# Finding the tokens of fixed expert items by comparisons and small products instead of a round trip through a slot table

## The chip, the cores and the metric

One core of a Trainium2 chip runs one program: three stages in a row, attention, a dense feed-forward layer and a top-1 mixture of experts. The metric is the device time of one execution in microseconds (us); lower is better. The profile is of one execution of the same program.

## The reference

Inputs are q, k, v of 2 batches x 8 heads x 576 positions x 64. The attention has a rotary position turn; its output is a matrix x of 1152 tokens x 512. The part that matters here is what follows the dense layer:

```python
x = _moe_ref(x, w_in, w_out)            # 1152 x 512 -> 2048 -> 512, gelu by sigmoid
logits = x @ w_gate                     # 8 experts
expert_idx = np.argmax(logits, axis=1)
gate_w = softmax(logits)[arange(N), expert_idx]
for i in range(N):                      # in order of the tokens
    e = expert_idx[i]
    if counts[e] < capacity:            # capacity = 288
        disp[e, counts[e]] = x[i]; pos[i] = counts[e]; counts[e] += 1; keep[i] = True
h = np.maximum(einsum('ecd,edf->ecf', disp, w1), 0)
y = einsum('ecf,efd->ecd', h, w2)       # 512 -> 1024 -> 512
out[i] = gate_w[i] * y[expert_idx[i], pos[i]] if keep[i] else 0
```

## The kernel before

**Matrix products.** A float32 operand is split into a rounded high part and a remainder (`hl[:, 0]`, `hl[:, 1]` for weights, `gh`, `gl` for activations), and each product is done three times: high by high, high by low, low by high. ScalarE writes the high part of a weight slice (L833), VectorE the low part (L834). A ring of four slices holds them.

**Order.** A planner orders the attention by hand. From the dense layer on the code is written in program order, and a scheduler that simulates the engines lays each engine's instructions out in one fixed sequence. Each engine works through its own sequence in order.

**Dense layer** (`first`, L904). The tokens go through in three chunks, 0 to 512, 512 to 768 and 768 to 1152 (`CUTS`). Each chunk makes 16 slices of the hidden layer: 12 products `h` (L853) and, two slices later, the products `y` (L883). The rows are written to a table in HBM, `x2`, one for each batch of 576 tokens.

**Routing** (`route`, L979). After the second chunk all tokens of batch 0 are known, after the third those of batch 1. For each batch some 60 small VectorE operations and six small products (`rank`, L1020 and L1023) give each token a slot number `lin`: the two largest groups of a batch become *items*. Four items are fixed: items 0 and 1 of batch 0 with 3 blocks of 96 and 2 blocks of 112 slots, items 2 and 3 of batch 1 with 3 blocks of 96 and 1 block of 96 (`STATIC`). What doesn't fit goes to surplus items, at most 16, in a loop at the end that runs `n - 4` times. In the profiled execution the loop doesn't run: there are nine gathers (L1146) and nine sends (L1193), one for each fixed block.

**The way from slot number to rows.** `route` casts `lin` to integers (`at`, L1056) and makes an `entry` for each token: its row in `x2` for the one batch and the other, its output row, its gate. Ten indirect DMAs issued by GpSimd (POOL in the profile; L1069, five for each batch, one for each tile of 128 tokens) scatter the entries into a table in HBM, `slots`. `gather` (L1136) reads an item's entries back (`ent`, L1141) and uses them as indices of an indirect DMA that fetches the tokens' rows (`got`, L1146; four buffers). `turn` (L1157) turns the rows on TensorE into `xt`.

**Experts** (`second`, L1205, for items 0 to 2; `few`, L1224, for item 3). Each item runs 8 slices through `h` and `y`; item 0 and 2 with 288 columns, item 1 with 224. A *hook* is a piece of work put into the sequence of slices: `turn(1)` and `turn(3)` four slices before the end of the items 0 and 2, `turn(2)` at the end of the last slice of item 1. The result `y` is copied to `yt` (L1213, one buffer), turned back (L1218), multiplied by the gate (L1221) and sent to the output rows by an indirect DMA (`send`, L1193). Which expert an item has is read from a small table `etab` that `route` fills after the slot numbers.

Of the kernel before, what the change touches and what calls it, by code (L numbers as in the profile page):

```python
# [25 lines left out]
P = 128  # L26
# [9 lines left out]
ROWS = 20  # L36
NSLOT = ITEMS * HALF
# [180 lines left out]
def consts():  # L218
# [18 lines left out]
    for b in range(B):  # L237
        rows[:, :, :, b] = np.where(batch == b, c, FAR)
    rows[:, :, :, 2] = batch * S + c
    masks = np.concatenate([valid.reshape(P, -1), (FAR * (1 - valid)).reshape(P, -1)], axis=1)  # L240
# [15 lines left out]
        "before": np.triu(np.ones((P, P), np.float32), 1),  # L256
        "small": np.repeat(small.astype(np.float32)[None], P, 0),
# [454 lines left out]
class Experts:  # L712
# [42 lines left out]
    def prepare(self):  # L755
# [19 lines left out]
        self.oh = one.tile([P, NC + 1, E], BF16, name="r_oh")  # L775
        self.small = one.tile([P, NC * E + 2 * ROWS * E + ROWS], F32, name="small")
# [202 lines left out]
    def route(self, b, L):  # L979
# [44 lines left out]
        rank, cnt = rank[:, 0:NC], rank[:, NC]  # L1024
        left, kc, items, key, base, at0 = (each(n) for n in ("left", "kc", "items", "key", "base", "at0"))
# [32 lines left out]
        ls, ex, sm, gate = big("ls"), big("ex"), col("sm"), col("gate")  # L1058
        tt(ls, L, per(mx), ALU.subtract)
        nc.scalar.activation(out=ex, in_=ls, func=AF.Exp)  # L1060
        red(sm, ex)
        ts(sm, sm, 1e-9, ALU.add)
        v.reciprocal(out=gate, in_=sm)
# [3 lines left out]
        done = []  # L1067
        for j in range(NC):
            ins = nc.gpsimd.indirect_dma_start(  # L1069
                out=self.slots,  # L1070
                out_offset=bass.IndirectOffsetOnAxis(ap=at[:, j:j + 1], axis=0),
                in_=entry[:, j, :],
                in_offset=None,
                bounds_check=NSLOT - 1,
                oob_is_err=False,
            )
            for x in done:
                self.tc.declare_no_dep(ins.ins, x.ins, reason="each token has a slot of its own")
            done.append(ins)
# [55 lines left out]

    def gather(self, item, batches, blocks=3, size=TT):  # L1136
# [6 lines left out]
        for i in range(blocks):  # L1143
            row = self.three.tile([P, DM], F32, name="got", bufs=4)[0:size]
            for b in batches:
                nc.gpsimd.indirect_dma_start(  # L1146
                    out=row,
                    out_offset=None,
                    in_=self.x2[b],
                    in_offset=bass.IndirectOffsetOnAxis(ap=ent[:, i, b:b + 1], axis=0),  # L1150
                    bounds_check=S - 1,
                    oob_is_err=False,
                )
# [51 lines left out]
    def second(self, ent, x, expert, hook=None):  # L1205
# [4 lines left out]
        y = self.ffn(x, [lambda f=f: self.slice_of(expert, f) for f in range(F2 // P)], self.relu, {hook[0]: hook[1]} if hook else {})  # L1210
# [96 lines left out]
    def run(self):  # L1307
        nc, tc = self.nc, self.tc
        sp = [mybir.EngineType.SP]
        found, x = {}, {}  # L1310

# [3 lines left out]
        def known(k):  # L1315
# [4 lines left out]
            for i in range(2 * b, 2 * b + 2):  # L1320
                found[i] = self.gather(i, [b], *STATIC[i])
# [8 lines left out]
        for i in range(3):  # L1330
            self.second(found[i][0], x[i], self.expert(i, sp), ((4, 0, 4)[i], lambda: turn(i + 1)))
        self.few(found[3][0], x[3], self.expert(3, sp))
        n = nc.values_load(self.etab[0:1, ITEMS:ITEMS + 1], min_val=4, max_val=ITEMS)
        with tc.If(n > 4, label="more"), tc.For_i(4, n, 1, iteration_sync="staggered") as i:
            ent, rows = self.gather(i, [0, 1])
            tc.stage_boundary()
            self.cut = []
            x = self.turn(rows, 0)
            tc.stage_boundary()
            self.second(ent, x, self.expert(i, sp))  # L1340
            tc.stage_boundary()
# [32 lines left out]
```

## Time and profile before

| what | value |
|---|---|
| runs of the program, median of 3 | 440.02 us (439.24 to 440.18) |
| the profiled execution, its own time | 437.69 us |
| its span, from the first to the last instruction | 436.0 us |
| granted TensorE clock, mean over the span | 0.998 of 2.4 GHz |
| busy: TensorE, VectorE, ScalarE, GpSimd | 97%, 75%, 61%, 31% |

The span is what the trace covers; 1.7 us of the execution's time lie around it. A stage is read by its times from the start of the span: the attention runs up to about 144 us, the three chunks of the dense layer to about 223, 268 and 336 us, items 0, 1 and 2 to about 367, 390 and 418 us, item 3 to the end. A matmul's row covers its way through the array, so neighbours overlap: its price is the distance from its start to the start of the next, not its duration.

### The profile page before, as it was taken

The page shows a single profiled execution, that of the slowest core. Times are in us where ns is not written, and L with a number is a line of the kernel's source. Part 1 is how long each engine was busy: PE and PEld are TensorE (multiplying, and loading weights), DVE is VectorE, ACT ScalarE, POOL GpSimd, SP SyncE. Part 2 cuts the span into 40 slices and gives each one's busy share as a digit, 9 for nine tenths or more (in the row PEclk, how much of TensorE's full clock was granted, in tenths as well). Part 3 has the DMA queues.
Part 4 walks back from the last instruction along what each step waited for, and adds up shares of the span by engine and source line. Part 5 has one row for each costly group of instructions (what it writes and reads, how often), then busy time and mean ns, then how long its engine had stood idle before and what let it go on. Part 6 is the DMA issues. An engine that isn't in the chain of part 4 may idle for free.

```text
span 436.0 us, 8504 instructions
## 1 busy us (share of the span) xinstructions
PE 423.7 (97%) x3150; PEld 349.5 (80%) x3150; DVE 326.0 (75%) x762; ACT 264.7 (61%) x556; POOL 137.2 (31%) x129
## 2 busy tenths in 40 slices
PE   7899999999999999999999999999999999999994
PEld 3566766666675888888899999898898999999992
DVE  5666766678998989997379988979546489766663
ACT  1798989988777334444456565574446356563662
POOL 1988778693347200000000000007330006531012
PEclk9999999999999999999999999999999999999999
DMA  8624413711343566665015000100824447686501
GB/s 269 234 114 153 152 47 107 250 30 50 98 161 114 194 214 213 238 234 208 2 72 208 34 3 0 50 0 1 291 76 135 154 144 181 199 273 221 213 21 53
DMA packets 20686, 58.96 MB, mean 135 GB/s; under 512 B 3542, under 2 KB 5910, under 8 KB 20641
## 3 DMA queue, kind: packets, MB, share of 16 engines
q1 hardware_dynamic: 18016, 53.98, 36.9%
q0 software_dynamic: 1664, 3.62, 2.8%
q10 hardware_dynamic: 960, 0.79, 0.5%
q8 instruction: 26, 0.43, 0.4%
q14 instruction: 20, 0.16, 0.1%
HBM read 51.79 MB, written 6.67 MB: 134 GB/s over the span
## 4 chain that ended last, share of the span: by engine, by line
PE 73%; issue 12%; DVE 4%; DMA 4%; POOL 3%; ACT 1%; SPq 0%; POOLq 0%; DVEq 0%; ACTq 0%
PE y L883 23%; PE h L853 23%; PE t L601 8%; PE s L488 7%; PE t L528 7%; PE s L477 2%; PE s L747 2%; POOL out L1193 2%; DMA turns<-in_turns 1%; DMA slots<-entry,r_at 1%; DMA wf<-in_w 1%; DVE pp L500 1%; POOL got L1146 1%; POOL slots L1069 1%; DVE hl L834 1%
## 5 line engine op out<-in xcount | busy, mean ns | idle before, releaser
L853 PE MATMUL h<-xt,hl 128*128 128x256 f32 (+4 forms) x828 | 145.7, 317 | 0.0
L853 PEld LDWEIGHTS h<-xt,hl 128*128 128x128 f32 x828 | 127.2, 189 | 9.9
L834 DVE TENSOR_TENSOR hl<-wf,hl 128x1024 fp32r<-128x1024 f32 x69 | 84.5, 1225 | 28.2 <-ACT hl L833 26.8
L833 ACT ACTIVATE hl<-wf 128x1024 fp32r<-128x1024 f32 x69 | 73.2, 1060 | 37.4 <-PE y L883 21.9
L883 PE MATMUL y<-hl,gh 128*128 128x512 f32 x288 | 82.6, 392 | 0.0
L1069 POOL DMA_INDIRECT slots<-entry,r_at x10 | 16.6, 1658 | 186.1 <-DVE r_ends L992 183.7
L883 PEld LDWEIGHTS y<-hl,gh 128*128 128x128 f32 x288 | 53.1, 188 | 9.6
L500 DVE TENSOR_SCALAR_CACHE_REDUCE pp<-s 128x576 f32<-128x576 f32 x64 | 46.0, 755 | 18.9 <-PE s L488 18.5
L893 ACT ACTIVATE g<-h 128x256 f32<-128x256 f32 (+2 forms) x45 | 21.8, 484 | 57.8 <-PE h L853 55.6
L512 ACT ACTIVATE pp<-pp,nm 128x576 f32<-128x576 f32 x64 | 49.2, 774 | 11.2 <-DVE pp L500 11.1
L461 POOL TENSOR_TENSOR qk<-qk,turns 128x640 f32<-128x640 f32 (+1 forms) x30 | 44.9, 1514 | 20.2 <-DMA qk<-in_qk 20.2
L883 PE MATMUL y<-hl,gl 128*128 128x512 f32 x144 | 49.7, 391 | 0.0
L488 PE MATMUL s<-qk 64*128 64x288 f32 x256 | 40.4, 421 | 1.3 <-DVE qk L463 0.7
L601 PE MATMUL t<-pt,vr 128*64 128x288 f32 x256 | 38.0, 417 | 0.0
L895 DVE TENSOR_TENSOR gl<-g,gh 128x512 fp32r<-128x512 f32 (+2 forms) x48 | 26.6, 559 | 13.1 <-ACT gh L894 12.6
L528 PEld LDWEIGHTS t<-ident,pp 64*128 64x128 f32 x576 | 25.8, 138 | 13.1 <-issue 4.2
L943 DVE SCALAR_TENSOR_TENSOR dot<-row,dots 128x512 f32<-128x512 f32 x48 | 32.9, 685 | 1.8 <-ACT row L931 1.4
L883 PE MATMUL y<-gh,hl 128*128 128x288 f32 (+1 forms) x192 | 33.4, 289 | 0.0
L407 ACT ACTIVATE pt<-t 128x512 f32<-128x512 f32 (+1 forms) x55 | 28.5, 542 | 6.7 <-PE t L528 6.4
L528 PE MATMUL t<-ident,pp 64*128 64x64 f32 x576 | 29.8, 228 | 1.6 <-ACT ptr L407 1.1
L883 PEld LDWEIGHTS y<-hl,gl 128*128 128x128 f32 x144 | 26.4, 188 | 4.3
L488 PEld LDWEIGHTS s<-qk 64*128 64x128 f32 x256 | 24.1, 188 | 6.1 <-DVE pp L500 1.6
(189 smaller groups left out, 583.7 us busy)
## 6 DMA issues: line engine op xcount, KB each, us to landing
wf<-in_w SPq DMA_DIRECT2D x32, 512.0 KB, 5.3
qk<-in_qk SPq DMA_DIRECT2D x14, 640.0 KB, 7.2
raw<-in_w_in SPq DMA_DIRECT2D x16, 512.0 KB, 4.4
raw<-in_w_out SPq DMA_DIRECT2D x16, 512.0 KB, 3.3
vr<-in_v SPq DMA_DIRECT2D x8, 320.0 KB, 4.9
out<-got SPq DMA_DIRECT2D x9, 256.0 KB, 3.7
dots<-in_w_dots SPq DMA_DIRECT2D x4, 512.0 KB, 4.5
x<-row SPq DMA_DIRECT2D x8, 256.0 KB, 3.4
```

The costliest lines, as they stand in the source:

```text
L407: return e.activation(out=out, in_=x, func=AF.Copy)
L461: e.tensor_tensor(out=u, in0=u, in1=self.turns[:, k, ts], op=ALU.mult)
L488: nc.tensor.matmul(both[h][:, n, 0:HALF], q[hs, at:at + P], k[hs, key:key + HALF], start=True, stop=True)
L500: self.nc.vector.tensor_scalar(out=self.room(p, i).rearrange("p (n k) -> p n k", n=2), in0=self.open.pop(("s", p, i))[:, :, 0:HALF], scala ...
L512: self.nc.scalar.activation(out=x, in_=x, func=AF.Exp, scale=-1.0, bias=self.nm[p % 2][:, i:i + 1], accum_out=self.sum[p % 2][:, i, 0:1],)
L528: self.nc.tensor.transpose(banks[b][:, at:at + 64], x[bs], self.ident[bs, bs])
L601: self.nc.tensor.matmul(o[h * 64:h * 64 + 64], x, y, start=j < 2, stop=j > 7)
L833: ins = nc.scalar.activation(out=hl[:, 0], in_=t, func=AF.Copy)
L834: self.last = nc.vector.tensor_tensor(out=hl[:, 1], in0=t, in1=hl[:, 0].bitcast(F32), op=ALU.subtract).ins
L853: ins = self.nc.tensor.matmul(h, u, v, start=m == 0, stop=m == len(ops) - 1)
L883: nc.tensor.matmul(y[j][:, 0:DM if rows else w], u, v, start=f == LAG and m == 0, stop=f == n + LAG - 1 and m == 2,)
L943: ins = nc.vector.scalar_tensor_tensor(out=self.weights.m2.tile([P, DM], F32, tag="m", name="dot"), in0=row, scalar=1.0, in1=self.dots[e], ...
```

## The change

Two constant tables are loaded in `setup`: `seats` (128 x 512 float32, each row 0 to 511) and `digits` (for each token its row number as a multiple of 32 and a remainder, and a constant; bfloat16). In `route` the gates are worked out ahead of the slot numbers. Then, for each batch:

- `mark` splits the gates into three bfloat16 parts in `digits` (four small VectorE operations) and compares `lin` with `seats`: five VectorE operations of 128 x 512 (batch 0) or 128 x 384 (batch 1), whose output `taken` is 1 where a token has a seat. The first four lie in the buffer of `yt`.
- `find` multiplies, for each block of seats, `taken` (stationary, 96 or 112 columns) with `digits` (6 columns), five products that add up: 25 for batch 0, 20 for batch 1. VectorE adds up the parts and makes `ents` of it, which has row number, output row and gate of every seat, and the rows are fetched from `x2` as before (`fetch`).
- `find(0)` stands in `route`, `find(1)` is a hook three slices before the end of item 0, behind `turn(1)`.
- The scatters and the reads of `ent` are no longer issued for the fixed items; all ten scatters (`scatter`) stand inside the `If` of the surplus items.

```diff
+SEATS = 512
+FIND = 3
+TURN = 0
...
+        self.seats = one.tile([P, SEATS], F32, name="seats")
+        self.digits = one.tile([P, B, NC, 6], BF16, name="digits")
...
+        load(self.seats, d["seats"])
...
+        digits = self.three.tile([P, DM], F32, name="got", bufs=4)[:, 0:3 * B * NC]
+        load(digits, d["digits"])
+        nc.vector.tensor_copy(out=self.digits[:, :, :, 0:3], in_=digits.rearrange("p (b k c) -> p b k c", b=B, c=3))
...
-        at = new("at", NC, dt=I32)
-        placed = v.tensor_copy(out=at, in_=lin)
+        placed = self.mark(b, lin, gate)
         self.placed = placed.ins.name
...
+        at = new(f"where{b}", NC, dt=I32)
+        v.tensor_copy(out=at, in_=lin)
...
-        for j in range(NC):
-            ins = nc.gpsimd.indirect_dma_start(
-                out=self.slots,
...
+        self.tokens.append((at, entry))
+        if b == 0:
+            self.find(b)
...
+    def mark(self, b, lin, gate):
...
+        v.tensor_copy(out=digits[:, :, 3], in_=gate)
+        v.tensor_tensor(out=rest, in0=gate, in1=digits[:, :, 3], op=ALU.subtract)
+        v.tensor_copy(out=digits[:, :, 4], in_=rest)
+        v.tensor_tensor(out=digits[:, :, 5], in0=rest, in1=digits[:, :, 4], op=ALU.subtract)
+        n = sum(math.prod(STATIC[i]) for i in (2 * b, 2 * b + 1))
+        room = self.two.tile([P, ND, HALF], F32, name="yt", bufs=1).rearrange("p j c -> p (j c)").bitcast(BF16)
+        last = self.one.tile([P, SEATS], BF16, name="taken")
+        for k in range(NC):
+            x = (room[:, k * SEATS:(k + 1) * SEATS] if k < NC - 1 else last)[:, 0:n]
+            ins = v.tensor_scalar(
+                out=x, in0=self.seats[:, 0:n], scalar1=lin[:, k:k + 1], scalar2=-2.0 * b * HALF,
+                op0=ALU.subtract, op1=ALU.is_equal,
+            )
...
+    def find(self, b):
+        groups = [(2, 3)] if b else [(0,), (1,)]
+        t = self.ps_m.tile([P, 512], F32, tag="m", name="who")
+        for items in groups:
...
+            for i in range(blocks):
+                for k in range(NC):
+                    x = self.taken[k][:, seat:seat + size]
+                    self.nc.tensor.matmul(u[:, i], x, digits[:, k], start=k == 0, stop=k == NC - 1)
...
+            v.tensor_reduce(out=total, in_=u.rearrange("p i (a c) -> p i a c", c=3), axis=AX.X, op=ALU.add)
+            for c, far in (0, FAR), (2, FAR + b * S):
+                v.tensor_scalar(out=ents[:, :, c], in0=total[:, :, 0], scalar1=float(far), scalar2=None, op0=ALU.add)
+            v.tensor_copy(out=ents[:, :, 3].bitcast(F32), in_=total[:, :, 1])
...
+                    self.fetch(row, b, ent[:, i, 0:1])
...
-            for i in range(2 * b, 2 * b + 2):
-                found[i] = self.gather(i, [b], *STATIC[i])
...
+            hooks = {(4, TURN, 4)[i]: lambda: turn(i + 1)}
+            if i == 0:
+                hooks[FIND] = lambda: self.find(1)
+            self.second(found[i][0], x[i], self.expert(i, sp), hooks)
...
+        with tc.If(n > 4, label="more"):
+            self.scatter()
```

## Rows read from the trace of the kernel before

**Rows 1.** First page, parts 1 and 2: busy time, and TensorE in 40 slices.
```profile
PE 423.7 (97%) x3150; PEld 349.5 (80%) x3150; DVE 326.0 (75%) x762; ACT 264.7 (61%) x556; POOL 137.2 (31%) x129
...
PE   7899999999999999999999999999999999999994
```
**Rows 2.** Stretches: busy us of each engine, granted clock, DMA share, GB/s.
```profile
265.00:336.00 71.00, 71.00 (x369) 63.97 (x367) 50.47 (x131) 40.28 (x61) 16.63 (x12) 1.00 0.25 79
336.00:390.00 54.00, 54.00 (x458) 53.73 (x457) 39.81 (x110) 28.69 (x47) 16.18 (x14) 1.00 0.61 189
390.00:418.00 28.00, 28.00 (x219) 28.00 (x218) 17.94 (x27) 15.13 (x30) 1.89 (x2) 1.00 0.55 190
418.00:430.20 12.20, 12.13 (x82) 9.89 (x80) 7.96 (x15) 7.07 (x19) 3.56 (x3) 1.00 0.14 41
...
345.00:367.00 22.00, 22.00 (x176) 21.93 (x177) 18.38 (x69) 11.00 (x17) 5.62 (x5) 1.00 0.47 126
```
**Rows 3.** Timeline of TensorE, runs of equal products in the third chunk: start, us.
```profile
264.96 0.51 PE L853 MATMUL h<-xt,hl 128*128 128x384 f32 x2
...
299.70 1.92 PE L853 MATMUL h<-xt,hl 128*128 128x384 f32 x10
301.45 0.63 PE L883 MATMUL y<-hl,gh 128*128 128x512 f32 x2
301.92 0.40 PE L883 MATMUL y<-hl,gl 128*128 128x512 f32 x1
```
**Rows 4.** The same in items 0 to 2.
```profile
335.87 0.42 PE L853 MATMUL h<-xt,hl 128*128 128x288 f32 x2
...
341.68 1.74 PE L853 MATMUL h<-xt,hl 128*128 128x288 f32 x12
343.26 0.95 PE L976 MATMUL tr<-gate,yt 128*128 128x8 f32 x8
344.07 1.04 PE L976 MATMUL tr<-gate,got 128*128 128x8 f32 x8
...
349.53 0.20 PE L1020 MATMUL rank<-r_oh,before 128*128 128x48 bf16 x1
349.57 0.27 PE L1023 MATMUL rank<-r_oh,ones 128*128 128x40 bf16 x5
349.70 0.58 PE L1164 MATMUL tg<-ident,got 112*128 112x112 f32 x4
350.05 0.38 PE L883 MATMUL y<-gh,hl 128*128 128x288 f32 x1
...
364.75 1.49 PE L853 MATMUL h<-xt,hl 128*128 128x224 f32 x12
366.08 1.22 PE L883 MATMUL y<-gh,hl 128*128 128x288 f32 x8
...
390.11 2.81 PE L853 MATMUL h<-xt,hl 128*128 128x288 f32 x20
...
418.07 1.83 PE L1251 MATMUL h<-hl,xt 128*96 128x256 f32 x14
```
**Rows 5.** Timeline of GpSimd, batch 1: from the scatters to the fetches.
```profile
360.16 1.01 POOL L1069 DMA_INDIRECT slots<-entry,r_at  x1 [31.90 <-DVE r_ends L992]
...
372.64 1.30 POOL L1141 DMA_DIRECT2D ent<-slots  x2 [4.53 <-DMA slots<-entry,r_at]
375.76 1.04 POOL L1146 DMA_INDIRECT got<-x,ent  x1 [1.82 <-PE h L853]
...
380.88 0.97 POOL L1146 DMA_INDIRECT got<-x,ent  x1 [0.30 <-issue]
```
**Rows 6.** Groups of VectorE instructions by shape: busy us, mean ns.
```profile
L703 DVE TENSOR_SCALAR m<-raw 128x512 uint32<-128x512 uint32 x32 | 13.8, 452 | 3.0 <-DMA raw<-in_w_out 2.9
...
L895 DVE TENSOR_TENSOR gl<-g,gh 128x384 fp32r<-128x384 f32 x16 | 8.8, 553 | 7.3 <-ACT gh L894 6.9 <-DVE hl L834 0.5
...
L1066 DVE COPY entry<-r_gate 128x5 f32<-128x5 f32 x2 | 0.3, 172 | 0.0
```
**Rows 7.** Timeline of VectorE at the end of item 0.
```profile
359.70 0.17 DVE L1056 CAST r_at<-r_lin 128x5 int32<-128x5 f32 x1
...
361.61 1.21 DVE L834 TENSOR_TENSOR hl<-wf,hl 128x1024 fp32r<-128x1024 f32 x1
```
**Rows 8.** Timeline of the SP queue in `setup`.
```profile
156.62 0.42 SPq L799 DMA_DIRECT2D got<-in_pad  x1
161.08 0.35 SPq L693 DMA_DIRECT2D raw<-in_w_out  x1
```

**Rows 9.** Timeline of the end, all engines.
```profile
430.17 0.68 ACT L1292 ACTIVATE row<-y,ent 96x512 f32<-96x512 f32 x1 [2.17 <-PE y L1282]
431.13 0.92 POOL L1193 DMA_INDIRECT out<-row,ent  x1 [1.70 <-ACT row L1292]
```

More of the change, by code (lines that the diff above doesn't have):

```diff
@@ L256, in consts @@
         "before": np.triu(np.ones((P, P), np.float32), 1),
+        "seats": np.repeat(np.arange(SEATS)[None], P, 0).astype(np.float32),
+        "digits": digits.reshape(P, -1).astype(np.float32),
         "small": np.repeat(small.astype(np.float32)[None], P, 0),
@@ L1024, in route @@
         rank, cnt = rank[:, 0:NC], rank[:, NC]
+        ls, ex, sm, gate = big("ls"), big("ex"), col("sm"), col(f"gate{b}")
+        tt(ls, L, per(mx), ALU.subtract)
+        nc.scalar.activation(out=ex, in_=ls, func=AF.Exp)
+        red(sm, ex)
+        ts(sm, sm, 1e-9, ALU.add)
+        v.reciprocal(out=gate, in_=sm)
         left, kc, items, key, base, at0 = (each(n) for n in ("left", "kc", "items", "key", "base", "at0"))
@@ new lines, in find @@
+    def find(self, b):
+        v, digits = self.nc.vector, self.digits[:, b]
+        groups = [(2, 3)] if b else [(0,), (1,)]
+        seat, column = 0, 0
+        t = self.ps_m.tile([P, 512], F32, tag="m", name="who")
+        for items in groups:
+            size = STATIC[items[0]][1]
+            blocks = sum(STATIC[i][0] for i in items)
+            u = t[0:size, column:column + 6 * blocks].rearrange("p (i c) -> p i c", c=6)
+            for i in range(blocks):
+                for k in range(NC):
+                    x = self.taken[k][:, seat:seat + size]
+                    self.nc.tensor.matmul(u[:, i], x, digits[:, k], start=k == 0, stop=k == NC - 1)
+                seat += size
+            column += 6 * blocks
+            total = self.one.tile([P, 4, 2], F32, name=f"total{items[0]}")[0:size, 0:blocks]
+            v.tensor_reduce(out=total, in_=u.rearrange("p i (a c) -> p i a c", c=3), axis=AX.X, op=ALU.add)
+            ents = self.one.tile([P, 4, 4], I32, name=f"found{items[0]}")[0:size, 0:blocks]
+            for c, far in (0, FAR), (2, FAR + b * S):
+                v.tensor_scalar(out=ents[:, :, c], in0=total[:, :, 0], scalar1=float(far), scalar2=None, op0=ALU.add)
+            v.tensor_copy(out=ents[:, :, 3].bitcast(F32), in_=total[:, :, 1])
+            at = 0
+            for item in items:
+                ent, rows = ents[:, at:at + STATIC[item][0]], []
+                at += STATIC[item][0]
+                for i in range(ent.shape[1]):
+                    row = self.three.tile([P, DM], F32, name="got", bufs=4)[0:size]
+                    self.fetch(row, b, ent[:, i, 0:1])
+                    rows.append(row)
+                self.found[item] = ent, rows
@@ new lines, in fetch, with scatter @@
+    def fetch(self, row, b, at):
+        self.nc.gpsimd.indirect_dma_start(
+            out=row,
+            out_offset=None,
+            in_=self.x2[b],
+            in_offset=bass.IndirectOffsetOnAxis(ap=at, axis=0),
+            bounds_check=S - 1,
+            oob_is_err=False,
+        )
+    def scatter(self):
+        nc, done = self.nc, []
+        for at, entry in self.tokens:
+            for j in range(NC):
+                ins = nc.gpsimd.indirect_dma_start(
+                    out=self.slots,
+                    out_offset=bass.IndirectOffsetOnAxis(ap=at[:, j:j + 1], axis=0),
+                    in_=entry[:, j, :],
+                    in_offset=None,
+                    bounds_check=NSLOT - 1,
+                    oob_is_err=False,
+                )
+                for x in done:
+                    self.tc.declare_no_dep(ins.ins, x.ins, reason="each token has a slot of its own")
+                done.append(ins)
@@ L1145, in gather @@
             for b in batches:
[L1146 to L1153, printed above, removed]
+                self.fetch(row, b, ent[:, i, b:b + 1])
             rows.append(row)
@@ L1203, in send, with second @@
         self.sent.append(ins)
-    def second(self, ent, x, expert, hook=None):
+    def second(self, ent, x, expert, hooks={}):
         nc = self.nc
@@ L1209, in second @@
         w = blocks * size
-        y = self.ffn(x, [lambda f=f: self.slice_of(expert, f) for f in range(F2 // P)], self.relu, {hook[0]: hook[1]} if hook else {})
+        y = self.ffn(x, [lambda f=f: self.slice_of(expert, f) for f in range(F2 // P)], self.relu, hooks)
         yt = self.two.tile([P, ND, HALF], F32, name="yt", bufs=1)
@@ L1310, in run @@
         found, x = {}, {}
+        self.found, self.tokens = found, []
         def turn(i):
```

39 lines of the change are left out of this document (14 added, 25 removed).

## The prediction, as it was made before the changed kernel ran

> **What bounds the kernel now.** I read the first page for the engines, then the stretches, then TensorE's timeline, and only then the chain that the change removes.
>
> The page shows TensorE busy for 97% of the span, and in its line of 40 slices nothing below 9 tenths from the second quarter to the last slice [rows 1]. The stretches from 265 to 418 us have no idle TensorE at all, the last one to 430.2 us 0.07 us [rows 2]. Since neighbouring matmuls overlap, "busy" could still hide waits, so I counted the work against the clock. A product costs what lies between its start and the next one's: 384 columns (301.45 - 299.70) / 10 = 0.175 us, 512 columns (301.92 - 301.45) / 2 = 0.235 us, rather 0.231 over longer runs [rows 3]; 288 columns (343.26 - 341.68) / 12 = 0.1317, 224 columns (366.08 - 364.75) / 12 = 0.111, a product with the gate weights (344.07 - 343.26) / 8 = 0.101, a transpose (350.05 - 349.70) / 4 = 0.0875, the six rank products together 0.17 us [rows 4].
>
> Third chunk: 192 products of 384 columns (33.6), 144 of 512 (33.3), the 12 left of the second chunk (2.8), 12 transposes (1.1) and one rank (0.2) make 71.0 us; it took 335.87 - 264.96 = 70.9 us [rows 3, 4]. Items 0 and 1: 192 products of 288 (25.3), 192 of 224 (21.3), 44 transposes (3.9), 24 gate products (2.4), rank (0.2) make 53.1 us; it took 390.11 - 335.87 = 54.2 us. Item 2: 192 of 288, 12 transposes and the first 12 products of item 3, priced like those of 224 columns (1.3), make 27.7 us; it took 27.96 [rows 4]. So TensorE's own work sets the time from 265 us to 430 us, and all its waits there are about 1.3 us, 1.1 of them in items 0 and 1. What follows the last product is a ScalarE row, its send and the landing [rows 9], which nothing in the diff touches.
>
> **The chain that goes away is beside this bound.** For batch 1 the slot numbers are ready at 359.9 us [rows 7], the scatters start at 360.16, the entries are read at 372.64, the fetches run from 375.76 to 381.9 us [rows 5]. The chain of work on the page runs through these instructions, because it follows the sends of GpSimd back; but TensorE has item 1 to do meanwhile and lost at most 1.1 us. For batch 0 the rows are wanted only by `turn(0)`, at the end of the third chunk, where the sum finds no wait. So 10 scatters and 4 reads less are worth between 0 and 1.1 us. I take 0: the 1.1 us is a difference of sums and no row shows TensorE waiting for a fetched row.
>
> **What is added on TensorE.** 25 + 20 = 45 products, in a stretch where TensorE has nothing free, so each adds its full price. No row shows a bfloat16 product with 96 or 112 stationary columns and 6 moving ones. The bounds are two rows: the five rank products with `ones`, bfloat16 and 128 columns, (349.70 - 349.57) / 5 = 0.026 us; and the gate products, float32, 128 stationary and 8 moving columns, 0.101 us [rows 4]. The first gives 45 x 0.026 = 1.2 us, the second 4.5 us. Which is nearer? Like the gate products each of the 45 has weights of its own and few moving columns, so that loading weights is the price; the five rank products load the same matrix five times, 128 wide. I take the gate product, scaled by stationary columns: 0.101 x 96 / 128 = 0.076 us for the 35 of 96 columns and 0.088 for the 10 of 112: 2.7 + 0.9 = 3.5 us. Both ends stay in the range.
>
> A rule to hold against it: the trace shows one bfloat16 weight load that is four times as quick as a float32 one [rows 4]. The Trainium skill, "TensorE: Matmul & The Clock Gate", section "Weight-path perf modes — Fast Weight Load (FWL) and DoubleRow", says that the quick load is switched on when there are 128 weights of a type that is not FP32. By that, blocks of 96 and 112 seats would not have it and the sum would stay near 3.5 us; by the rank row alone it would be 1.2 us. No row here has a bfloat16 load of fewer than 128 columns, so the trace does not decide it.
>
> **What is added on VectorE.** `mark`: four small operations at 0.17 us or less each [rows 6], and five comparisons. A comparison of 512 float32 elements against a per-row scalar lies between L703 (512 elements, 0.45 us) and the one-element-a-cycle pace of L895 (384 elements, 0.55 us, so about 0.7 for 512) [rows 6]: 2.3 to 3.5 us for batch 0 and 1.7 to 2.8 for batch 1. `find` adds a reduction and three small operations for each of three groups, 0.7 us a group. For batch 0 that is up to 5.6 us in the third chunk, where VectorE is idle 71.0 - 50.5 = 20.5 us [rows 2]: nothing. For batch 1 it is 3.1 to 4.2 us where VectorE is busy 18.4 of 22 us [rows 2], idle 3.6. The first thing made late is the low half of the next weights, L834 at 361.61, which ends at 362.82 and is wanted by item 1's first product at 364.75 us [rows 4, 7]: 1.9 us of cover. The five comparisons stand ahead of it by up to 2.8 us if the scheduler puts them all there, 1.7 at the low end. The four gate operations need only the gates, which are ready long before, and the sums of `find` come after the 20 products, behind that slice. I take 0, near the low end because the comparison is the same kind of operation as L703, and keep 0.9 us of stall, the excess over the cover, for the range. The expert table is filled after the marks; it is later by the same 2 to 3 us.
>
> **What is added elsewhere.** `seats` (256 KB) and `digits` on the SP queue during `setup`: there the queue stands from 156.62 to 161.08 us because it waits for a buffer [rows 8]; its neighbours are issued in about 0.4 us each, so two more fit into those 4.0 us. If the transfer pushed back the one that frees the buffer, the dense layer's weights would be late; the TensorE line shows no wait there that it would add to [rows 1], and I take 0. `find` holds one of the two small PSUM buffers and, until its products are done, the buffer of `yt`; item 0 copies to `yt` only at the end of its slices, some 4 us after `find(1)` can have run. The fetches keep their four buffers: the fifth of batch 0 still waits for `turn(0)`, as before, and nothing that is wanted sooner stands behind it on GpSimd. The `If` holds ten DMAs more that aren't reached.
>
> **Sum.** 3.5 us on TensorE, 0 elsewhere: the profiled execution goes from 437.7 to 441.2 us, its span from 436.0 to 439.5. The median of the runs shown lies 440.0 - 437.7 = 2.3 us above that execution, so the runs should give 443.5 us.
>
> **Rivals.**
> *Quick weight loads.* The 45 products cost 0.026 us each: +1.2 us, 441.2. For it: same type as the rank products. Against it: other widths, new weights each time. It may end on either side of the border of "no change"; about 0.9 us, 0.2%, is what a measurement of this kernel tells from nothing.
> *VectorE becomes the bound in item 0.* If the comparisons run at 0.55 us and stand ahead of L834, or if TensorE reaches the products of `find(1)` before the last mark is written (each engine works in a fixed order, so all of item 0 would wait behind them), TensorE stands 1 to 3 us on top of 3.5: 444.5 to 446.5. Deciding point: more than 1.9 us of new VectorE work ahead of L834.
> *Nothing to see.* The 45 products at 0.026 us take the place of 1.1 us of waits in items 0 and 1 that were for late rows: 0.1 us, 440.1. Here the change does what it says, and the end is the same.
> *Faster.* TensorE's waits in items 0 and 1 were for fetched rows, and the products of `find` fall into waits that are left in the third chunk and items 0 to 2, which together are about 1.3 us. Then it gains up to 1.3 us: 438.7. It decides only if nearly all those 1.3 us were waits, and the products cost next to nothing on top. Against it: the sums above match with prices from undisturbed rows.
>
> **How the numbers follow.** Slow weight loads, my forecast: 0.45, own range 442.3 to 444.6. Quick loads: 0.23, of which two thirds slower by over 0.2% and one third within. VectorE: 0.12. Nothing to see: 0.10. Faster: 0.10, most but not all of it by more than 0.2%. That makes slower 0.45 + 0.15 + 0.12 = 0.72, same 0.08 + 0.10 + 0.01 = 0.19, faster 0.09. The range leaves out the faster case and the worst of the VectorE case: 439.8 to 446.0 us.
>
> **What would show it.** In the profile after: ten L1069 rows and four `ent` rows gone; the fetches of batch 1 some ten us earlier and turn(2) without effect; 45 new products in two groups, whose start-to-start distance is 0.076 us or 0.026; item 0 longer by 20 of them, the third chunk by 25; TensorE without a gap before the groups; L834 behind the second marks still ahead of its product. I am wrong if TensorE shows idle time ahead of the new products, if their price is near 0.03 us, or if items 0 and 1 together get shorter than 54.2 us.

## The result, and the profile after

The median of six runs is 442.31 us (441.67 to 443.70); six runs of the kernel before beside them gave 439.14 us (438.08 to 440.18). The ratio is 1.0075 with an interval of 1.0051 to 1.0099: the change costs 3.2 us. (A ratio here is estimated from all the undisturbed runs, so it need not be the quotient of the two medians.) The profiled execution took 441.81 us (before: 437.69), its span is 440.0 us (before: 436.0).

Part 1 and the TensorE line of the first page of the kernel after, against [rows 1]:

```profile
PE 426.0 (97%) x3195; PEld 351.9 (80%) x3195; DVE 332.0 (75%) x793; ACT 264.8 (60%) x556; POOL 121.5 (28%) x115
...
PE   7899999999999999999999999999999999999993
```

There are 45 matmuls more and 14 GpSimd instructions fewer, as the diff says. TensorE is as full as before; GpSimd is 15.7 us less busy, and the program is longer. The stretches of the kernel after, with the columns of [rows 2] (busy us of each engine, granted clock, DMA share, GB/s), cut at the same events:

```profile
265.00:337.60 72.60, 72.60 (x394) 65.32 (x392) 53.42 (x148) 40.15 (x61) 6.97 (x5) 1.00 0.24 77
337.60:393.00 55.40, 55.40 (x480) 55.09 (x479) 42.46 (x124) 28.75 (x47) 10.00 (x7) 1.00 0.58 187
393.00:420.90 27.90, 27.90 (x218) 27.90 (x218) 17.83 (x26) 15.03 (x29) 1.88 (x2) 1.00 0.52 182
345.00:369.00 24.00, 24.00 (x205) 23.89 (x204) 20.15 (x80) 12.16 (x17) 0.01 (x1) 1.00 0.37 116
420.90:433.00 12.10, 12.02 (x82) 9.78 (x80) 7.86 (x15) 6.97 (x19) 3.55 (x3) 1.00 0.14 40
```

TensorE has no idle time in the stretches that grew, and the granted clock is 1.00 in all of them. So the place to look is the distances between fixed events on its timeline. I take five: the start of the third chunk, the first product of item 0, the first product of item 3, the last product, the start of the last send, and then the end of the span (printed to 0.1 us, so the last two columns hold to about that). This table holds them for every kernel of this study (us; the difference to before in brackets):

| kernel | third chunk starts | third chunk | items 0 to 2 | item 3 to last product | to last send | last send to end | span |
|---|---|---|---|---|---|---|---|
| before | 264.96 | 70.91 | 79.19 | 14.67 | 1.40 | 4.87 | 436.0 |
| after | 264.95 | 72.49 (+1.58) | 80.42 (+1.23) | 14.66 | 1.40 | 6.08 (+1.21) | 440.0 |
| e1_nine_products | 264.95 | 71.24 (+0.33) | 79.46 (+0.27) | 14.69 | 1.39 | 5.57 (+0.70) | 437.3 |
| e2_before_and_45 | 265.30 | 72.08 (+1.17) | 80.17 (+0.98) | 14.67 | 1.40 | 4.88 | 438.5 |
| e3_last_first | 265.21 | 72.21 (+1.30) | 80.16 (+0.97) | 14.68 | 1.39 | 6.15 (+1.28) | 439.8 |
| e4_empty_surplus | 265.55 | 72.49 (+1.58) | 80.41 (+1.22) | 14.67 | 1.38 | 4.80 | 439.3 |
| e5_128_wide | 265.06 | 71.92 (+1.01) | 79.81 (+0.62) | 14.67 | 1.39 | 6.15 (+1.28) | 439.0 |
| e8_before_long_branch | 268.93 | 70.90 | 79.20 | 14.67 | 1.39 | 7.41 (+2.54) | 442.5 |
| e9_branch_twice | 266.93 | 72.48 (+1.57) | 80.41 (+1.22) | 14.67 | 1.39 | 6.12 (+1.25) | 442.0 |
| e10_cheapest | 265.20 | 71.93 (+1.02) | 79.82 (+0.63) | 14.66 | 1.39 | 4.80 | 437.8 |

How to read it: where two kernels have the same code in a stage (before and e8, or after, e4 and e9), the stage agrees to 0.02 us, far finer than the medians of whole runs. The start of the third chunk, in contrast, moves between 264.95 and 268.93 from one profiled execution to another, and e8, which has the kernel before up to the surplus branch, moves the most (its mean granted clock is 0.987, against 0.998 before and 0.996 after; in its first 80 us it is 0.96, against 1.00 in both). That shift arises ahead of the stages where the change does its work, and it goes into every run's time. In the two profiles of before and after it happens to be equal, so their spans differ by what the change costs: 1.58 + 1.23 + 1.21 = 4.0 us. The medians, over executions that start the third chunk at different times, give 3.2 us with an interval of 2.2 to 4.3, in which 4.0 lies. Because of that spread the fastest runs follow the table better than the medians do: in the two later rounds the fastest run of before took 437.82 us (beside e1 to e4) and 437.65 us (beside e5 to e10), and those of e1 to e4 lie 1.2, 2.0, 3.6 and 2.4 us above it, those of e5, e8, e9 and e10 3.0, 2.5, 4.0 and 1.5 us.

**The products of `find`.** TensorE's timeline of the kernel after, around the two groups for batch 0 (the first figure of a line is its start):

```profile
299.66 0.86 PE L865 MATMUL h<-xt,hl 128*128 128x384 f32 x4
300.36 0.17 PE L1173 MATMUL who<-digits,yt 128*96 128x6 bf16 x1
300.39 0.42 PE L865 MATMUL h<-xt,hl 128*128 128x384 f32 x1
300.65 0.17 PE L1173 MATMUL who<-digits,yt 128*96 128x6 bf16 x1
300.67 0.42 PE L865 MATMUL h<-xt,hl 128*128 128x384 f32 x1
...
301.51 0.17 PE L1173 MATMUL who<-digits,taken 128*96 128x6 bf16 x1
301.53 0.32 PE L1173 MATMUL who<-digits,yt 128*96 128x6 bf16 x4
301.71 0.18 PE L1173 MATMUL who<-digits,taken 128*96 128x6 bf16 x1
301.76 0.32 PE L1173 MATMUL who<-digits,yt 128*96 128x6 bf16 x4
301.94 0.18 PE L1173 MATMUL who<-digits,taken 128*96 128x6 bf16 x1
301.98 0.95 PE L865 MATMUL h<-xt,hl 128*128 128x384 f32 x4
302.77 0.63 PE L895 MATMUL y<-hl,gh 128*128 128x512 f32 x2
...
307.49 0.33 PE L1173 MATMUL who<-digits,yt 128*112 128x6 bf16 x4
...
307.98 1.31 PE L865 MATMUL h<-xt,hl 128*128 128x384 f32 x6
```

Durations of 0.17 to 0.33 us mislead here, because neighbours overlap. Start to start, a group of five with 96 columns costs 301.76 - 301.53 = 0.23 us, 0.046 each (0.044 in e3), and ten with 112 columns cost 307.98 - 307.49 = 0.49, 0.049 each. But the first four don't lie together: each stands alone between float32 products. From 300.36 to 301.51 there are four of them and four products of 384 columns, which cost 4 x 0.175 = 0.70 [rows 3]; 0.45 is left, 0.11 us for each lone one. All 25 cost 0.45 + 0.47 + 0.49 = 1.41 us of the chunk's 1.58. In item 0, read the same way, the 20 cost 1.14 us of 1.23.

The lines also show where the price of a lone product lies, and the 0.26 us that are left. A lone product starts only 0.02 to 0.03 us ahead of the float32 product behind it; it is that float32 product which takes 0.26 us to the next start (300.39 to 300.65) instead of 0.175. The first float32 product behind a whole group is late in the same way: the four from 301.98 take 302.77 - 301.98 = 0.79 us instead of 0.70. In every kernel of this study the first product `h` or `y` behind bfloat16 products, one or a group, takes 0.08 to 0.09 us longer. In the kernel after there are three groups, and three times that is the 0.26 us.

**VectorE.** Its timeline in the kernel after, when batch 1 is routed, against [rows 7]:

```profile
361.29 1.41 DVE L1153 TENSOR_SCALAR yt<-seats,r_lin 128x384 bf16<-128x384 f32 x4
362.61 0.41 DVE L1153 TENSOR_SCALAR taken<-seats,r_lin 128x384 bf16<-128x384 f32 x1
...
363.98 1.21 DVE L846 TENSOR_TENSOR hl<-wf,hl 128x1024 fp32r<-128x1024 f32 x1
```

Five comparisons of 384 take 1.7 us, and the low half of the weights (L846) ends at 365.2 us, 3.4 us ahead of item 1's first product at 368.60. The first product of `find(1)` starts at 364.36, 1.3 us after the last mark.

**GpSimd.** Its timeline in the kernel after: the fetches of batch 1, and the end, against [rows 5, 9]:

```profile
368.99 1.92 POOL L1193 DMA_INDIRECT got<-x,found  x1 [38.91 <-DVE r_n L1004]
...
373.75 1.53 POOL L1193 DMA_INDIRECT got<-x,found  x1 [0.30 <-issue]
...
433.92 0.92 POOL L1268 DMA_INDIRECT out<-row,found  x1 [1.70 <-ACT row L1367]
```

The fetches run from 368.99 to 375.28 us where they ran from 375.76 to 381.9. The rows are asked for 6.8 us sooner; e2 and e3 below show what that is worth.

**The end.** After the last send comes what the forecast counted at nothing. These are the instructions of line 1411, the `If`, in the kernel after; the columns are count, then duration in ns as min/median/max, then first and last start in us:

```profile
L1411 POOLq EVENT_SEMAPHORE  x4: 17/43/1637, 435.2 to 435.4; - x4
...
L1411 PEldq COMPARE_BRANCH  x1: 3782/3782/3782, 432.9 to 432.9; - x1
...
L1411 POOLq COMPARE_BRANCH  x1: 45/45/45, 434.7 to 434.7; - x1
L1411 POOLq INC_SWDGE_SEM  x1: 539/539/539, 437.1 to 437.1; - x1
```

And the program's last line in the same kernel:

```profile
L1449 POOLq DRAIN  x3: 45/107/1527, 437.7 to 439.8; - x3
```

(POOLq is GpSimd's instruction queue, PEldq TensorE's.) The branch isn't taken, but GpSimd's queue has four semaphore instructions and one `INC_SWDGE_SEM` on the way past it. In the trace they name semaphores 111 to 118, the eight that GpSimd's DMAs raise. The longest wait lasts from 435.42 to 437.06 us, and it ends with the landing of the last send: that send's semaphore, 112, gets the last of its updates at 437.03. `INC_SWDGE_SEM` lasts until 437.64, and towards its end each of the eight semaphores is updated once more (437.54 to 437.60). Only then does the drain begin, which lasts until 439.2. In the kernel before, the `If` (L1334) and the last line (L1370) have these rows for GpSimd:

```profile
L1334 POOLq COMPARE_BRANCH  x1: 50/50/50, 431.9 to 431.9; - x1
```

```profile
L1370 POOLq DRAIN  x3: 46/103/3123, 432.1 to 435.7; - x3
```

There the branch is one instruction on GpSimd's queue, and the drain starts 1.0 us after the start of the last send and is through 4.1 us after it (431.13 to 435.2). In the kernel after it is through 5.3 us after that start (433.92 to 439.2). That is the 1.2 us. The last send's semaphores split it: the send lands 2.7 us after its start in the kernel before and 3.1 in the kernel after, and from the landing to the end of the drain it is 1.4 us before and 2.2 after.

### The profile page after: what moved, and what is told of

Read it like the earlier page. It is cut to its first block, busy times and chain, and to the rows that moved or that the text cites. A ratio compares the mean times of both kernels' runs of the same rounds, so it can differ in the third digit from the quotient of the medians.

```text
span 440.0 us, 8593 instructions
## 1 busy us (share of the span) xinstructions
PE 426.0 (97%) x3195; PEld 351.9 (80%) x3195; DVE 332.0 (75%) x793; ACT 264.8 (60%) x556; POOL 121.5 (28%) x115
## 4 chain that ended last, share of the span: by engine, by line
PE 79%; issue 12%; DVE 4%; POOL 1%; DMA 1%; ACT 1%; SPq 0%; POOLq 0%; DVEq 0%
PE y L895 26%; PE h L865 25%; PE t L607 8%; PE s L494 7%; PE t L534 6%; PE s L483 2%; PE s L753 2%; POOL out L1268 1%; DMA turns<-in_turns 1%; DVE pp L506 1%; PE tr L988 1%; DVE pt L414 0%; PE tg L1239 0%; PE who L1173 0%; DVE prem L506 0%
## 5 line engine op out<-in xcount | busy, mean ns | idle before, releaser
L846 DVE TENSOR_TENSOR hl<-wf,hl 128x1024 fp32r<-128x1024 f32 x69 | 84.3, 1223 | 24.4 <-ACT hl L845 24.3
L895 PE MATMUL y<-hl,gh 128*128 128x512 f32 x288 | 83.6, 391 | 0.0
L1193 POOL DMA_INDIRECT got<-x,found x9 | 12.3, 1372 | 218.6 <-DVE found L1181 160.5
L895 PE MATMUL y<-hl,gl 128*128 128x512 f32 x144 | 50.7, 392 | 0.0
L895 PE MATMUL y<-gh,hl 128*128 128x288 f32 (+1 forms) x192 | 34.4, 291 | 0.0
```

What stands on the lines that cost most here:

```text
L846: self.last = nc.vector.tensor_tensor(out=hl[:, 1], in0=t, in1=hl[:, 0].bitcast(F32), op=ALU.subtract).ins
L895: nc.tensor.matmul(y[j][:, 0:DM if rows else w], u, v, start=f == LAG and m == 0, stop=f == n + LAG - 1 and m == 2,)
```

## The experiments

### e1_nine_products: one product for each block instead of five

```diff
-                for k in range(NC):
-                    x = self.taken[k][:, seat:seat + size]
-                    self.nc.tensor.matmul(u[:, i], x, digits[:, k], start=k == 0, stop=k == NC - 1)
+                x = self.taken[0][:, seat:seat + size]
+                self.nc.tensor.matmul(u[:, i], x, digits[:, 0], start=True, stop=True)
```

> The changed kernel with one product for each block of seats instead of five: 9 products for 45; the five comparisons and everything else stay. It leaves out the tokens of four of five tiles when it looks up seats, so most seats stay empty. Theory (the products on TensorE are the price, 2.55 us of the 3.2): 36 products less are worth 1.8 to 2.1 us, so the end is about 1.2 us after the kernel before. Rival (the comparisons on VectorE, the loads or the end of the program are the price): the end stays about 3 us after the kernel before.

It leaves out the tokens of four of five tiles, so most seats stay empty. Median 439.18 us beside 439.33 of before, ratio 0.9981 (0.9945 to 1.0017): by the medians not to be told from before. The expected 1.2 us does not show there; it shows in the profiled executions (span 437.3 us against 436.0). From the start of the third chunk to the last product it takes 165.39 us, 2.18 less than after, for 36 products: 0.061 each. The ten comparisons on VectorE are all still there, and with nine products left the two stages are only 0.60 us above before. In the trace the nine take 0.36 us and the three late float32 products behind their groups 0.25: that is the 0.60. So the products carry the stages' cost, and the marks nothing that can be seen.

### e2_before_and_45: the kernel before, with 45 such products and nothing else

```diff
+        who = self.ps_m.tile([P, 512], F32, tag="m", name="who")
+        for i, size in enumerate(((96, 96, 96, 112, 112), (96, 96, 96, 96))[b]):
+            for k in range(NC):
+                nc.tensor.matmul(
+                    who[0:size, 6 * i:6 * i + 6], self.before[:, 0:size], oh[:, k, 0:6], start=k == 0, stop=k == NC - 1
+                )
```

> The kernel before, with its scatters, reads and fetches as they were, and 45 products more on TensorE of the same shapes (25 in the routing of batch 0, 20 in that of batch 1; stationary a constant matrix of 96 or 112 columns, moving 6 columns), whose results nobody reads. Theory (the products are the price, and the chain of scatters was hidden and is worth nothing): 45 x 0.045 = 2.0 us slower than the kernel before, up to 2.6 if some are interleaved. Rival (quick loads for a matrix loaded again and again): 45 x 0.026 = 1.2 us. Rival (the chain was worth something that the change won back): this kernel is slower than the changed one, by up to 1.1 us.

Median 440.53 us, ratio 1.0018 (0.9984 to 1.0051); the stages grow by 1.17 + 0.98 = 2.15 us, as the theory expected (2.0 to 2.6). TensorE's timeline of this kernel:

```profile
290.74 1.33 PE L1060 MATMUL who<-r_oh,before 128*96 128x6 bf16 x25
291.93 0.78 PE L853 MATMUL h<-xt,hl 128*128 128x384 f32 x3
...
351.21 1.04 PE L1060 MATMUL who<-r_oh,before 128*96 128x6 bf16 x20
352.12 0.52 PE L853 MATMUL h<-xt,hl 128*128 128x288 f32 x2
```

25 products in 1.19 us are 0.048 each, and the 20 in item 0, all with 96 columns, 0.046 each, although all of them load the same matrix as weights, cut to 96 or 112 columns. They stand behind the rank products, so they add no group of their own. "New weights each time", which the forecast held against the cheap price, isn't what makes them dear. And the scatters are all still issued here: this kernel is a control for the removed chain, used under e3.

### e3_last_first: the sum starts with the fifth tile of tokens

The fifth mark (`taken`) is the last that VectorE writes; the products of a block now begin with it.

```diff
-                for k in range(NC):
+                for k in reversed(range(NC)):
                     x = self.taken[k][:, seat:seat + size]
-                    self.nc.tensor.matmul(u[:, i], x, digits[:, k], start=k == 0, stop=k == NC - 1)
+                    self.nc.tensor.matmul(u[:, i], x, digits[:, k], start=k == NC - 1, stop=k == 0)
```

> The changed kernel with the five products of a block in the order of tiles 4 to 0. The first product needs the last comparison, so the scheduler puts the products of a batch together instead of one by one between the float32 products. Theory (a product alone between float32 products costs about 0.11 us, one behind its like 0.045): nine of the ten lone products get cheaper by about 0.065 us, 0.6 us in all; TensorE's last product is at 432.3 us of the span or earlier where it was at 432.9. Rival (the price of one is the same wherever it stands): no change.

Median 442.04 us, ratio 1.0060 (1.0033 to 1.0086). The lone products are gone; TensorE's timeline of this kernel has one run for each group:

```profile
302.15 0.17 PE L1173 MATMUL who<-digits,taken 128*96 128x6 bf16 x1
302.18 0.32 PE L1173 MATMUL who<-digits,yt 128*96 128x6 bf16 x4
302.36 0.18 PE L1173 MATMUL who<-digits,taken 128*96 128x6 bf16 x1
302.40 0.32 PE L1173 MATMUL who<-digits,yt 128*96 128x6 bf16 x4
```

The stages are 0.28 and 0.26 us shorter than after. Eight lone products at 0.11 instead of 0.045 are 0.52 us, and 0.54 came back (the expectation counted nine and 0.6). Compare it with e2, which has as many products together and keeps the whole scatter chain: items 0 to 2 take 80.16 us without the chain and 80.17 with it. Batch 1's shorter route is worth nothing; a gain that the marks on VectorE happened to eat up is ruled out as far as e1 shows that the marks cost nothing.

### e4_empty_surplus: no scatters in the branch

The line `self.scatter()` under the `If` is left out, so that surplus items would have no entries; in these runs there are none.

> The changed kernel without the ten scatters inside the branch for surplus items, which isn't taken here; surplus items, of which there are none, would lack their entries. In the profiled executions the stretch from the start of the last send to the end of the span is 4.87 us before and 6.08 us after. Theory (that stretch differs from run to run, it has nothing to do with the change): same time as the changed kernel, within 0.9 us. Rival (stepping over a longer branch costs at the end of the program): 1.2 us faster than the changed kernel.

Median 441.12 us, ratio 1.0042 (1.0013 to 1.0071). The stages are those of after to 0.01 us, and the end takes 4.80 us, about what it takes before. The expectation's theory, that the end has nothing to do with the change, is refuted. The `If` of this kernel, all engines that have a large row:

```profile
L1411 PEldq COMPARE_BRANCH  x1: 3818/3818/3818, 433.5 to 433.5; - x1
...
L1411 POOLq COMPARE_BRANCH  x1: 45/45/45, 435.3 to 435.3; - x1
```

The semaphore instructions and `INC_SWDGE_SEM` are gone. The 3.8 us that TensorE's queue spends at the branch, against 0.46 us in the kernel before, are still there and cost nothing, so they aren't the reason. The last send lands 3.1 us after its start, as in the kernel after, but the drain is through 0.8 us behind the landing instead of 2.2. The end of the program is 1.3 to 1.4 us longer because of ten DMAs that aren't issued.

### e5_128_wide: blocks of 128 stationary columns

Each block loads 128 columns from its first seat, and only its own rows of the result are used; the last block of batch 0 keeps its 112. The order is that of e3, and the marks of batch 1 are 416 wide.

```diff
-        n = sum(math.prod(STATIC[i]) for i in (2 * b, 2 * b + 1))
+        n = 416 if b else 512
...
+                last = b == 0 and seat + P > SEATS
+                for k in reversed(range(NC)):
+                    x = self.taken[k][:, seat:seat + (size if last else P)]
+                    y = t[0:size if last else P, column + 6 * i:column + 6 * i + 6]
+                    self.nc.tensor.matmul(y, x, digits[:, k], start=k == NC - 1, stop=k == 0)
```

> The changed kernel with the products of a block in the order of tiles 4 to 0 and with 128 stationary columns instead of 96 or 112, of which the upper ones belong to the next block and aren't read (the last block of batch 0 keeps its 112; the comparisons of batch 1 are 416 wide instead of 384). Theory (a bfloat16 load of 128 columns is the quick one, as in the rank products): 40 of the 45 products at 0.026 us instead of 0.045, the third chunk 0.4 us and items 0 and 1 0.4 us shorter than with the order alone; about 1.2 us of products in all. Rival (the load takes a clock for each column): 0.060 us each, 0.6 us longer than with the order alone.

Median 441.66 us, ratio 1.0067 (1.0045 to 1.0088). TensorE's timeline of this kernel, first the three blocks of item 0, then the two of item 1, one 128 wide and one 112:

```profile
302.13 0.17 PE L1175 MATMUL who<-digits,taken 128*128 128x6 bf16 x1
302.16 0.24 PE L1175 MATMUL who<-digits,yt 128*128 128x6 bf16 x4
302.26 0.17 PE L1175 MATMUL who<-digits,taken 128*128 128x6 bf16 x1
302.29 0.24 PE L1175 MATMUL who<-digits,yt 128*128 128x6 bf16 x4
302.39 2.36 PE L865 MATMUL h<-xt,hl 128*128 128x384 f32 x12
...
308.60 0.18 PE L1175 MATMUL who<-digits,taken 128*128 128x6 bf16 x1
308.64 0.24 PE L1175 MATMUL who<-digits,yt 128*128 128x6 bf16 x4
308.75 0.19 PE L1175 MATMUL who<-digits,taken 128*112 128x6 bf16 x1
308.80 0.35 PE L1175 MATMUL who<-digits,yt 128*112 128x6 bf16 x4
309.00 0.77 PE L865 MATMUL h<-xt,hl 128*128 128x384 f32 x3
```

Five products with 128 columns cost 302.26 - 302.13 = 0.13 us, 0.026 each: the price of the rank products [rows 4], in a place where the weights are new each time. The five with 112 columns beside them cost 309.00 - 308.75 = 0.25 us, 0.050 each. More columns are cheaper. Against e3 the stages are 0.29 and 0.35 us shorter; 20 products at 0.045 - 0.026 would be 0.38 in each. The rival, 0.6 us longer, is refuted.

### e8_before_long_branch: the kernel before, with ten DMAs in the branch

The ten scatters of the kernel before stay where they are, and ten more that never run (those of batch 1, twice) are put into the `If`.

```diff
-        with tc.If(n > 4, label="more"), tc.For_i(4, n, 1, iteration_sync="staggered") as i:
-            ent, rows = self.gather(i, [0, 1])
...
+        with tc.If(n > 4, label="more"):
+            self.scatter()
+            with tc.For_i(4, n, 1, iteration_sync="staggered") as i:
+                ent, rows = self.gather(i, [0, 1])
```

> The kernel before with ten more indirect DMAs inside the branch for surplus items, which isn't taken; nothing else. Theory (the longer branch makes the end of the program longer: 4.80 to 4.88 us from the last send's start to the end of the span in three kernels without scatters in it, 5.57 to 6.15 in three with them): about 6.1 us there, and a time 1.2 us above the kernel before. Rival (the last send's landing varies for another reason that the change brings, as the indices being in another place): 4.9 us, no change.

Median 442.80 us beside 438.50 of before, ratio 1.0073 (1.0045 to 1.0100). All stages up to the last send are those of before to 0.01 us; the end takes 7.41 us, 2.54 more, twice what was expected. GpSimd's rows at the `If` of this kernel:

```profile
L1352 POOLq EVENT_SEMAPHORE  x4: 17/43/43, 436.1 to 438.0; - x4
...
L1352 POOLq INC_SWDGE_SEM  x1: 826/826/826, 438.1 to 438.1; - x1
```

and at its last line:

```profile
L1390 POOLq DRAIN  x3: 46/103/2677, 439.0 to 442.2; - x3
```

The same instructions appear as in the kernel after, so DMAs in a branch that isn't taken are enough to make them. The wait for the last send's landing is there too, but as a gap ahead of the fourth semaphore instruction (436.25 to 438.02 us; the send lands at 438.00), and the drain is through 3.6 us behind the landing instead of 1.4 in the kernel before. (The span of this execution is long for another reason as well: its third chunk begins 4.0 us late.) `INC_SWDGE_SEM` takes 0.83 us instead of 0.54 and the drain 2.68 instead of 1.53; why they are longer here stays open.

### e9_branch_twice: twenty DMAs in the branch

The kernel after, with `self.scatter()` written twice under the `If`.

> The changed kernel with the ten scatters inside the branch written twice; it isn't taken. Theory (it is the length of what is stepped over): the stretch from the last send to the end grows past 6.1 us, by up to another 1.2 us. Rival (a step: the target lies out of reach or it doesn't): it stays at 6.1 us. Second rival (nothing to do with the branch): anywhere between 4.8 and 6.1.

Median 442.31 us, ratio 1.0081 (1.0057 to 1.0105); the end takes 6.12 us against 6.08 with ten. GpSimd's rows at the `If`:

```profile
L1411 POOLq EVENT_SEMAPHORE  x4: 17/43/1662, 437.1 to 437.4; - x4
...
L1411 POOLq INC_SWDGE_SEM  x1: 539/539/539, 439.1 to 439.1; - x1
```

One `INC_SWDGE_SEM` of 539 ns serves twenty as it serves ten. The cost is a step: having such DMAs in the branch or not, not how many, and so not the length of the code that is jumped over.

### e10_cheapest: 128 wide, together, and no scatters in the branch

The edits of e5 and e4 together.

> The changed kernel with the order of tiles 4 to 0, 128 stationary columns, and no scatters in the branch (surplus items, of which there are none, would lack their entries). If products and branch are all that the change costs, 45 products at the quick price are left: 1.2 to 1.4 us slower than the kernel before, with 4.8 us from the last send to the end. If loads by column are the rule, 2.5 us slower.

Median 439.60 us beside 438.50, ratio 1.0020 (1.0000 to 1.0041). Both savings add up: the stages are those of e5, the end that of e4. What is left is 1.02 + 0.63 = 1.65 us of TensorE time, more than the 1.2 to 1.4 expected: the products take 1.3, and the three late float32 products behind their groups, which the expectation left out, 0.26. No version that was tried and finds all tokens beats the kernel before; as long as the products stand in TensorE's full stretch, the shorter chain gives nothing to set against them.

## Why the prediction was right, and where its sum was not

The forecast was 443.5 us, 3.5 above the median that it started from; the runs gave 442.31, 3.2 above the median beside them. The side, the size and the main mechanism hold. Inside the sum two terms are off, in opposite directions.

1. **"TensorE's own work sets the time from 265 us to 430 us."** Held. TensorE has no idle time in the stretches that grew, and e2, which only adds products, lengthens the stages by 2.15 of the 2.81 us. Leaving out 36 products in e1 takes 2.18 of them back.
2. **The scatter chain is beside the bound; worth 0, at most 1.1 us.** Held at 0: 80.17 us with the chain (e2), 80.16 without (e3). The 1.1 us left over in the sum for items 0 and 1 was no wait for rows. The fetches of batch 1 start 6.8 us sooner, where the forecast said some ten.
3. **45 products at 0.076 and 0.088 us: 3.5 us.** This is the term that was mis-sized. It measured 2.8 us. The step that failed is the scaling of the float32 gate product by columns: among its like a bfloat16 product with 96 columns costs 0.045, with 112 columns 0.049. To that come eleven float32 products, one behind each of the eight lone products and the three groups, that are 0.08 to 0.09 us late, 0.9 us in all, which the forecast did not think of. "Their price is near 0.03" was one of its signs of being wrong, and 0.045 lies nearer to that than to 0.076; only with the late products does the mean come to 2.8 / 45 = 0.062. The reason it gave, weights that are new each time, is refuted by e2: the same matrix over and over costs 0.048. The other bound, 0.026, is the price at 128 columns, with new weights too (e5). The rule of the Trainium skill that was weighed there ("TensorE: Matmul & The Clock Gate", section "Weight-path perf modes — Fast Weight Load (FWL) and DoubleRow") speaks of 128 weights of a type that is not FP32 as the condition for quick loading. The rows agree with the condition: 0.026 at 128 columns, 0.050 at 112 in the same run. As by that rule, blocks of 96 and 112 cost more than blocks of 128, but the dear bound was not their price.
4. **VectorE: 0, with 0.9 us of stall kept for the range.** Held. The comparisons of 512 took 0.40 us each from start to start, 0.33 at 384, below the cheap bound L703 [rows 6]. The five for batch 1 took 1.7 us, and L846 had 3.4 us to spare where the forecast counted on 1.9. The first product of `find(1)` did not wait for a mark.
5. **The two loads in `setup`: 0.** No cost shows: the third chunk starts at 264.95 us in the kernel after and 264.96 in the one before, and over all profiled executions at 264.95 to 266.93 us with the loads, 264.96 to 268.93 without. A shift below the spread between executions could not be seen.
6. **"The `If` holds ten DMAs more that aren't reached", and "What follows the last product ... nothing in the diff touches".** Failed. The end is 1.2 us longer. Removing the DMAs from the branch takes it away (e4, e10), putting DMAs into the branch of the kernel before brings it on (e8), and doubling them changes nothing (e9). The trace names the instructions: a wait for the last send's landing and `INC_SWDGE_SEM` ahead of the drain, on the path that does not take the branch. By the split above 0.8 of the 1.2 us lie behind the landing, and 0.4 are a later landing that e4 has as well. A rival in e4's expectation, that a longer branch costs something at the end, was right about the place and wrong about the reason: it isn't length.
7. **The sum.** 2.8 + 1.2 = 4.0 us in the profiled pair instead of 3.5. The offset from the profiled execution to the median came out at 0.5 us for the kernel after (442.31 - 441.81), not 2.3: the runs of before lay 0.4 to 2.5 us above its profiled execution, those of the kernel after between 0.1 below and 1.9 above. So the product term was 0.7 us too large, the end 1.2 missing and the offset 1.8 too large. That 443.5 came within 1.2 us of the result is partly luck: terms that were too large stood in for one that was missing.

Of the rivals, quick weight loads would have needed 128 columns; VectorE did not become the bound; "nothing to see" and "faster" both needed waits for rows that did not exist.

What was not settled: why `INC_SWDGE_SEM` and the drain take longer in e8, and why the last send lands 3.1 us after its start in the kernels after and e4, where it lands after 2.7 us in before and e2. In e4 a shorter stretch behind the landing (0.8 us against 1.4 before) makes up for it. Why the first float32 product behind bfloat16 ones is late no run shows, only that it is.

## What to carry to other kernels

Shortening a chain is worth what an engine waits for it; when the sum of prices fills the critical engine's time, extra products there cost their full price however long the chain that they replace, so count the waits first. Price a small product by type and number of stationary columns from start-to-start distances, make a bfloat16 block with few moving columns 128 wide even if some columns are useless, and let it start with the operand that is ready last so that the group stays together: each return from bfloat16 to float32 is paid for as well. Treat DMAs of GpSimd moved into a branch that is rarely taken as a cost on the other path too, above all where the branch stands at the end of the program.

## What the runs showed of the hardware that was not expected

- **A branch not taken with GpSimd DMAs in it is not free.** GpSimd's queue first waits until the last send has landed, then has one `INC_SWDGE_SEM` (0.54 us, 0.83 in e8), and only then the drain: 1.3 to 1.4 us at this program's end (after against e4) and 2.5 us in e8 against before, the same for ten DMAs and for twenty.
- **Fewer stationary columns can cost more.** With 6 moving columns a bfloat16 product costs 0.026 us at 128 stationary columns and 0.044 to 0.050 at 96 and 112, with the same weights each time or new ones.
- **Going back from bfloat16 to float32 costs 0.08 to 0.09 us.** The first float32 product `h` or `y` behind bfloat16 ones takes that much longer to the next start, behind one product as behind twenty. So a single one between two float32 products costs 0.11 us in all, more than twice what it costs among its like. Written in an order in which the last operand comes last, eight of them slipped out of their groups, for 0.5 us.
- **A median in the list of DMA issues can rest on two or three transfers.** For the fetches it went from 4.2 us in the kernel before to 7.5 us after, but the trace tells the landing of only two of nine before and three after: there two of batch 0 took 7.5 and 7.7 us, one of batch 1 3.5 us. It does not show that fetches became slower in general, and no engine was waiting for them.
